# Float32 weights straight from the load for the second MoE's groups of 128 rows

## The chip, the cores and the metric

The kernel runs on one core of a Trainium2 chip. The metric is the device time of one execution in microseconds, the median of several runs; lower is better.

## The reference

Three layers stand one behind the other. The first is windowed attention with 4 batches, 8 heads, 576 positions and head size 64; its output is read as x with 2304 rows of 512. The second is a dense MoE layer, softplus(x @ w_in) @ w_out with an inner width of 2048. The third is a top-2 MoE with 8 experts of inner width 1024, and this is the one that the change is about:

```python
for e in range(E):
    for k in range(2):
        mask = top2[:, k] == e
        if not mask.any():
            continue
        h = np.maximum(x[mask] @ w1[e], 0.0)
        out[mask] += top2_w[mask, k, None] * (h @ w2[e])
```

`w1[e]` is 512 x 1024 and `w2[e]` is 1024 x 512, both float32, 2 MB each. Every row of x goes to its two best experts, weighted by `top2_w`.

## The kernel before

**Stages.** Attention is interleaved with the first MoE, which works through 9 chunks of 256 rows; each chunk is also routed (logits, top 2, rank in its expert's list), and each row's number and weight go into a table in DRAM, `rect`, by expert. Then the second MoE works through groups of rows that share an expert. A group of 256 rows is a *pair*, a group of 128 rows a *single*. There are 18 pairs (3 early ones and 15 late ones) and 5 singles that always run; two more singles stand under a condition at the end and do not run here. The order of the late ones is two pairs, a single, then three times three pairs and a single, then four pairs and the last single.

**Splitting.** To keep float32 precision, a matmul in the format float32r is done on split operands: a value is written as a high part, rounded to float32r, and a low part, the rest. high x high, high x low and low x high are added up: three matmuls for one product. Weights come by DMA as float32 into one of 4 raw buffers (`raw2`, 128 x 1024, 512 KB, `w2_load`); `w2_split` turns each into two ring tiles (`w_tile`, 128 x 2 x 512, 512 KB each). The high part of each half is copied by ACT (L1067), the low part is a subtraction (L1068), for the first half on POOL once the first MoE has freed its weights, for the second on DVE. The ring has 24 slots (`NRING`) of the same size as a raw buffer. A group needs 8 loads and so 16 ring tiles.

**A pair.** `g_rows` reads the group's part of `rect` (`rc`, L975, 4 buffers), `g_gather` fetches its rows with an indirect DMA from POOL's queue (`xg`, L984), `g_transpose` turns them over on TensorE (L199), ACT and DVE evict them as `xh` and `xl` (L999, L1000). For each of 8 steps f, `s1` makes one h tile of 128 x 256 (12 matmuls of 256 columns, the weights stationary), ACT and DVE evict it as `gh` and `gl` (L1100, L1101), and two steps later `s3` adds six matmuls of 512 columns to the two y (or z) tiles. At the end ACT and DVE evict these with the row weight as scale (`ys`, L1168, L1171), and POOL scatters them with an indirect DMA that adds to `out` (L1162), one DMA for each 128 rows.

**A single.** It has two steps of 512 columns. `s1` uses the transposed rows as the stationary operand and the weights as the moving one: 4 blocks of the contraction, 3 matmuls of 512 columns each, 12 in a step. ACT evicts h with the ReLU as `hs` (L1117), `s2` turns it over with 4 transposes, ACT and DVE split it into `th` and `tlo` (L1133, L1134), and `s3` adds 12 matmuls of 512 columns to y or z.

**What sets the order.** The program is written out in one order for each engine, by the class `Order`: TensorE's work is written down step by step, its cost is added to a planned time, and chains of steps for the other engines are put into their queues when the planned time reaches them. The costs in it are the author's figures and set the order alone. Each engine, and SP's queue of DMA issues, then works through its queue strictly in order. `pump` is called whenever a ring tile has been used up (`w2_free`): it loads while a raw buffer is free (`w2_load`), and splits while the ring has room for two tiles (`w2_split`). The pieces are taken in the order of the list `WJ`. A load into a raw buffer waits for the split of the piece that was in it, four pieces before; the high copy into a ring slot waits for the matmul that read it last. A row list `rc` waits for the scatter of the group four before it, which read the same buffer. PSUM has 2 h buffers, and the transposes share the t buffers with z.

The matmuls are all issued by one line, L188 in `mm`, so the groups of the profile are told apart by tiles: `h<-w,xh` with 512 columns is a single's up-projection, `y<-w,th` and `z<-w,th` its down-projection, `h<-xh,w` with 256 columns a pair's (or the first MoE's) up-projection.

Of the kernel before, what the change touches and what calls it, by code (L numbers as in the profile page):

```python
# [18 lines left out]
P = 128  # L19
# [76 lines left out]
def ca(n):  # L96
    return 0.06 + n * 0.000833
# [15 lines left out]
def moe_chain_kernel(ctx, tc, qk, v, w_in, w_out, w_gate, w_noise, noise, w1, w2, out):  # L113
# [875 lines left out]
    def g_transpose(g, a):  # L989
        n, eo, i = groups[g]  # L990
        d = GR[g]
        pt = ps_t(("gx", g, a)).rearrange("p (c t) -> p c t", c=KC)
        for kc in range(KC):
            tr(pt[:, kc, :], d["xg"][a][:, kc * P:(kc + 1) * P], ident)
        if a == 0:
            d["xT"] = tuple(tl(mid, [P, KC, CT], F32R, x, 2, ("gup", g)) for x in ("xh", "xl"))
        xh, xl = d["xT"]
        sl = slice(a * P, (a + 1) * P)
        chain(("A", ca(512), lambda: ACT.activation(xh[:, :, sl], pt, AF.Copy)),  # L999
              ("V", cv(512), lambda: DVE.tensor_sub(xl[:, :, sl], pt, f32(xh[:, :, sl])), ("gx", g, a)))  # L1000
# [3 lines left out]
    for g, (n, eo, i) in enumerate(groups):  # L1004
# [3 lines left out]
        else:  # L1008
            WJ += [(g, 0, f) for f in range(NF1 // 2)] + [(g, 1, f) for f in range(NF1 // 2)]
    NW = len(WJ)  # L1010
    wl, wsp = [0], [0]
    REG, W2, RAW2 = {}, {}, {}
    NRAW2 = 4
    freed = [0]
    nslot = [0]

    def w2_load():
        j = wl[0]
        if j >= NW or (j >= NRAW2 and ("w2", j - NRAW2) not in o_.fin):
            return False  # L1020
        g, kind, f = WJ[j]
        if g >= sure[0] or ("tab", int(g >= NEARLY)) not in o_.fin:
            return False
        wl[0] += 1
        n, eo, i = groups[g]
        if g not in REG:
            REG[g] = SP.value_load(TB[eo][0:1, 0, i:i + 1], min_val=0, max_val=E - 1)
            if g >= NEARLY:
                g_rows(g)
            chain(("P", 1.1 * n, lambda: g_gather(g), ("gg", g)), (None, 2.2, None, ("gl", g)), after=4.0)  # L1030
        e = bass.ds(REG[g], 1)
        raw = tl(p2, [P, 1024], F32, "raw2", NRAW2, ("w2", j))
        chain(("DMA", (1 << 19) / 330e3, None), (None, 2.0, None, ("r2", j)))
        if kind == 1:
            SP.dma_start(raw.rearrange("p (a n) -> p a n", a=2),
                         w2[e, f * 256:(f + 1) * 256, :].rearrange("e (a p) n -> p (e a) n", p=P))
        elif n == 2:
            SP.dma_start(raw.rearrange("p (c f) -> p c f", c=KC),
                         w1[e, :, f * 256:(f + 1) * 256].rearrange("e (c p) f -> p (e c) f", p=P))
        else:  # L1040
            h, c0 = divmod(f, 2)
            SP.dma_start(raw.rearrange("p (c f) -> p c f", c=2),
                         w1[e, c0 * 256:(c0 + 1) * 256, h * 512:(h + 1) * 512]
                         .rearrange("e (c p) f -> p (e c) f", p=P))
        RAW2[j] = raw
        return True

    def w2_split():
        j = wsp[0]
        if j >= wl[0] or sptr[0] < len(suses) or live1() + nslot[0] + 2 - freed[0] > NRING:  # L1050
            return False
        wsp[0] += 1
        nslot[0] += 2
        g, kind, f = WJ[j]
        n = groups[g][0]
        raw = RAW2.pop(j)
        for a in range(2):
            t = W2[g, kind, 2 * f + a] = w_tile()
            if kind == 0 and n == 2:
                src = raw.rearrange("p (c a f) -> p c a f", c=KC, a=2)[:, :, a, :]  # L1060
                hi, lo = (t[:, z].rearrange("p (c f) -> p c f", c=KC) for z in range(2))
            else:
                src, hi, lo = raw[:, a * 512:(a + 1) * 512], t[:, 0], t[:, 1]
            key = ("w2", j) if a else ("w2a", j)
            on_v = a or live1() > 0
            sub = ("V", cv(512)) if on_v else ("P", cg(512))
            chain(("A", ca(512), lambda hi=hi, src=src: ACT.activation(hi, src, AF.Copy), None, (("r2", j),)),  # L1067
                  sub + (lambda e=DVE if on_v else POOL, hi=hi, lo=lo, src=src: e.tensor_tensor(  # L1068
                      lo, src, f32(hi), OP.subtract), key))
        return True  # L1070
# [19 lines left out]
    def s1(g, f):  # L1090
        n = groups[g][0]
        if n == 2:
            need(("w2" if f % 2 else "w2a", WJ.index((g, 0, f // 2))))
            for a in range(2):
                need(("gx", g, a))
            ph = up(W2[g, 0, f], GR[g]["xT"], CT, ("hr2", g, f))
            w2_free()
            gh = tl(mid, [P, CT], F32R, "gh", 4, ("dn", g, f))
            gl = tl(mid, [P, CT], F32R, "gl", 4, ("dn", g, f))
            chain(("A", ca(CT), lambda: ACT.activation(gh, ph, AF.Relu)),  # L1100
                  ("V", cv(CT), lambda: DVE.scalar_tensor_tensor(gl, ph, 0.0, f32(gh), op0=OP.max, op1=OP.subtract),  # L1101
                   ("hr2", g, f)))
            H2[g, f] = (gh, gl)
        else:
            need(("gx", g, 0))
            ph = tl(psum, [P, 512], F32, "h", 2, ("hr2", g, f))
            xh, xl = GR[g]["xT"]
            x = 0
            for kc in range(KC):
                need(("w2" if kc % 2 else "w2a", WJ.index((g, 0, 2 * f + kc // 2))))  # L1110
                w = W2[g, 0, 4 * f + kc]
                for l, r in ((xh, 0), (xh, 1), (xl, 0)):
                    mm(ph, l[:, kc, :P], w[:, r, :], x == 0, x == 3 * KC - 1)
                    x += 1
                w2_free()
            hs = tl(p2, [P, 512], F32, "hs", 2, ("ht", g, f))
            chain(("A", ca(512), lambda: ACT.activation(hs, ph, AF.Relu), ("hr2", g, f)))  # L1117
            H2[g, f] = hs
        if f == (NF1 if n == 2 else 2) - 1:
            mark(("gup", g))  # L1120

    def s2(g, f):
# [5 lines left out]
        for x in range(4):  # L1128
            tr(pt[:, x, :], hs[:, x * P:(x + 1) * P], ident)
        mark(("ht", g, f))  # L1130
        th = tl(p2, [P, 4, P], F32R, "th", 2, ("dn", g, f))
        tlo = tl(p2, [P, 4, P], F32R, "tlo", 2, ("dn", g, f))
        chain(("A", ca(512), lambda: ACT.activation(th, pt, AF.Copy)),  # L1133
              ("V", cv(512), lambda: DVE.tensor_sub(tlo, pt, f32(th)), ("hT", g, f)))  # L1134
        H2[g, f] = (th, tlo)

    def s3(g, f):
        n = groups[g][0]
# [8 lines left out]
            w2_free()  # L1147
        else:
            need(("hT", g, f))
            th, tlo = H2.pop((g, f))  # L1150
            for x in range(4):
                ff = 4 * f + x
                need(("w2" if ff % 2 else "w2a", WJ.index((g, 1, ff // 2))))
                down(Y2[g], th[:, x, :], tlo[:, x, :], W2[g, 1, ff], ff == 0, ff == NF1 - 1)
                w2_free()
        mark(("dn", g, f))
        if f == (NF1 if n == 2 else 2) - 1:
            rc = GR[g]["rc"]
# [180 lines left out]
```

## Time and profile before

| | |
|---|---|
| median of 3 runs | 1256.97 us (1254.11 to 1257.41) |
| the profiled execution, its own time | 1252.39 us |
| its span, first to last instruction | 1250.5 us |
| mean granted TensorE clock | 0.948 |
| TensorE matmul, weight load | 1104.3 us (88%), 929.4 us (74%) |
| VectorE, ScalarE, GpSimd | 877.1 us (70%), 655.9 us (52%), 734.6 us (59%) |
| DMA | 237.19 MB, mean 190 GB/s |

The second MoE has TensorE to itself from about 700 us on; the last matmul ends near 1238 us. Busy shares are means over the whole program. In the profile PE is TensorE's matmuls and PEld its weight loads, DVE is VectorE, ACT ScalarE, POOL GpSimd and SP the queue that issues most DMAs. A line of time gives the start, the duration, the engine, the line of the kernel, the operation with its tiles, how many were merged, and in brackets how long the engine stood idle before it and what the profile takes for the cause. A group line gives the count, the busy time, the mean of one in ns, and the idle time before. Where a wait is put down to an engine that had long been done, another cause is meant, often a DMA.

### The profile page before, as it was taken

To read this page: it belongs to the slowest core of one execution; us is meant where nothing else is said; L and a number is where in the kernel's file an instruction comes from. 1 tells how busy PE (TensorE), PEld (TensorE's weight loads), DVE (VectorE), ACT (ScalarE), POOL (GpSimd) and SP (SyncE) were. 2 spreads that over 40 slices of the span, in tenths; PEclk is the share of its full clock that TensorE was granted. 3 is DMA by queue.
4 is the path that set the end of the run, shared out by engine and by line. 5 is a ranking of instruction groups with operands and counts; after the bars stand their busy time and mean duration, and the time that the engine had idled before them with its cause. 6 is when DMAs were issued, how large, how long until landed. Compare 5 with 4: busy or idle time off the path is not lost. (4 is left out here: it accounts for less than half of the span.)

```text
span 1250.5 us, 21557 instructions
## 1 busy us (share of the span) xinstructions
PE 1104.3 (88%) x7021; PEld 929.4 (74%) x7021; DVE 877.1 (70%) x2136; ACT 655.9 (52%) x1653; POOL 734.6 (59%) x718
## 2 busy tenths in 40 slices
PE   5567689998999999999998987987987988988996
PEld 3445467877878778888876887977977977977884
DVE  8999999675677776767588775755655655655671
ACT  6655455554545455555355534555655554654651
POOL 4666666455464646565554546666567566576661
PEclk8778879999999999999999998998998998998998
DMA  5465434367757555555585558678678677787762
GB/s 211 154 190 186 143 102 137 124 192 240 253 185 253 182 194 186 194 157 169 181 281 163 167 128 236 170 233 245 176 231 237 185 235 221 200 234 210 211 164 27
DMA packets 138068, 237.19 MB, mean 190 GB/s; under 512 B 18336, under 2 KB 73760, under 8 KB 137952
## 3 DMA queue, kind: packets, MB, share of 16 engines
q1 hardware_dynamic: 127616, 214.24, 53.6%
q0 software_dynamic: 10336, 21.54, 8.8%
q8 instruction: 57, 0.93, 0.3%
q14 instruction: 59, 0.48, 0.1%
HBM read 205.41 MB, written 30.33 MB: 189 GB/s over the span
## 5 line engine op out<-in xcount | busy, mean ns | idle before, releaser
L188 PE MATMUL h<-xh,w 128*128 128x256 f32 x2304 | 485.0, 293 | 63.0 <-DVE gl L1101 36.9
L188 PEld LDWEIGHTS h<-xh,w 128*128 128x128 f32 x2304 | 388.7, 196 | 95.5 <-DVE gl L1101 41.3
L1068 DVE TENSOR_TENSOR w<-raw,w 128x512 fp32r<-128x512 f32 x197 | 241.5, 1229 | 164.1 <-ACT w L1067 153.0
L188 PE MATMUL h<-xl,w 128*128 128x256 f32 x1152 | 333.1, 289 | 15.0 <-DVE xl L423 10.5
L1067 ACT ACTIVATE w<-raw 128x512 fp32r<-128x512 f32 x368 | 221.5, 627 | 157.8 <-DMA raw<-in_moe_w 105.9
L1068 POOL TENSOR_TENSOR w<-raw,w 128x512 fp32r<-128x512 f32 x171 | 234.8, 1443 | 89.5 <-ACT w L1067 86.1
L188 PE MATMUL y<-w,gh 128*128 128x512 f32 x736 | 243.8, 413 | 6.0 <-DVE gh L556 6.0
L188 PEld LDWEIGHTS h<-xl,w 128*128 128x128 f32 x1152 | 226.3, 196 | 24.2 <-DVE xl L423 11.3
L559 POOL TENSOR_TENSOR su<-sa,su 128x256 f32<-128x256 f32 x144 | 108.0, 750 | 120.2 <-DVE su L558 90.3
L188 PEld LDWEIGHTS y<-w,gh 128*128 128x128 f32 x736 | 127.7, 193 | 33.6 <-issue 8.2
L188 PE MATMUL y<-w,gl 128*128 128x512 f32 x368 | 146.1, 397 | 0.7 <-DVE gl L557 0.7
L551 ACT ACTIVATE sa<-h 128x256 f32<-128x256 f32 x144 | 54.7, 380 | 165.4 <-PE h L188 139.6
L1162 POOL DMA_INDIRECT out<-ys,rc x41 | 70.0, 1708 | 117.9 <-PE h L188 39.2
L188 PE MATMUL z<-w,gh 128*128 128x512 f32 x416 | 139.1, 417 | 0.0
L555 POOL TENSOR_TENSOR sl<-sl,su 128x256 f32<-128x256 f32 x144 | 110.2, 766 | 19.0 <-DVE sl L554 4.6
L556 DVE CAST gh<-sl 128x256 fp32r<-128x256 f32 x144 | 62.6, 435 | 76.1 <-POOL sl L555 76.1
L364 POOL TENSOR_TENSOR s<-s,st 128x512 f32<-128x512 f32 (+2 forms) x80 | 80.2, 1007 | 53.0 <-DVE st L361 25.0
L355 ACT ACTIVATE s<-s,st 128x256 f32<-128x256 f32 (+2 forms) x160 | 76.2, 478 | 62.5 <-DVE st L351 62.5
L1100 ACT ACTIVATE gh<-h 128x256 fp32r<-128x256 f32 x144 | 54.7, 380 | 93.2 <-PE h L188 65.3
L188 PE MATMUL z<-w,gl 128*128 128x512 f32 x208 | 84.2, 405 | 3.1 <-DVE gl L557 3.1
L188 PEld LDWEIGHTS y<-w,gl 128*128 128x128 f32 x368 | 70.4, 191 | 18.2 <-DVE gl L557 2.0
L557 DVE TENSOR_TENSOR gl<-sl,gh 128x256 fp32r<-128x256 f32 x144 | 81.6, 568 | 3.1
(235 smaller groups left out, 1646.1 us busy)
## 6 DMA issues: line engine op xcount, KB each, us to landing
raw<-in_moe_w SPq DMA_DIRECT2D x184, 512.0 KB, 4.8
w<-scratch SPq DMA_DIRECT2D x126, 512.0 KB, 4.7
qkT<-in_qk SPq DMA_DIRECT2D x20, 512.0 KB, 6.1
scratch<-w SPq DMA_DIRECT2D x18, 512.0 KB, 3.1
raw<-in_moe_w_in SPq DMA_DIRECT2D x16, 512.0 KB, 5.6
raw<-in_moe_w_out SPq DMA_DIRECT2D x16, 512.0 KB, 6.1
out<-zero SPq DMA_DIRECT2D x19, 256.0 KB, 6.0
x1buf<-x SPq DMA_DIRECT2D x9, 512.0 KB, 4.5
```

Of the source, the lines that this page charges most:

```text
L188: PE.matmul(o, l, r, start=start, stop=stop)
L355: ACT.activation(s[:nq, j, :n], s[:nq, j, :n], AF.Exp, bias=st[:nq, j:j + 1], scale=-1.0, accum_out=st[:nq, 2 + j:3 + j])
L364: POOL.tensor_tensor(s[:nq, :, :n], s[:nq, :, :n], st[:nq, 6:8, None].to_broadcast([nq, 2, n]), OP.mult)
L551: chain(("A", ca(CT), lambda: ACT.activation(a, ph, AF.Abs)), ("A", ca(CT), lambda: ACT.activation(a, a, AF.Exp, scale=-1.0), ("e", t)), ( ...
L555: ("P", cg(CT), lambda: POOL.tensor_add(l, l, u), None, (("d", t),)),
L556: ("V", cv2(CT), lambda: DVE.tensor_copy(gh, l)),
L557: ("V", cv(CT), lambda: DVE.tensor_sub(gl, l, f32(gh)), ("g", t)))
L559: ("P", cg(CT), lambda: POOL.tensor_tensor(u, a, u, OP.subtract), ("d", t)), after=2 * ca(CT) + 0.15)
L1067: chain(("A", ca(512), lambda hi=hi, src=src: ACT.activation(hi, src, AF.Copy), None, (("r2", j),)), sub + (lambda e=DVE if on_v else POOL ...
L1068: sub + (lambda e=DVE if on_v else POOL, hi=hi, lo=lo, src=src: e.tensor_tensor(lo, src, f32(hi), OP.subtract), key))
L1100: chain(("A", ca(CT), lambda: ACT.activation(gh, ph, AF.Relu)), ("V", cv(CT), lambda: DVE.scalar_tensor_tensor(gl, ph, 0.0, f32(gh), op0=O ...
L1162: POOL.indirect_dma_start(out=out[:, :], out_offset=bass.IndirectOffsetOnAxis(ap=rc[:, a, 0:1], axis=0), in_=ys, in_offset=None, compute_o ...
```

## The change

Singles no longer split anything. Their weights are loaded as float32 straight into a ring slot (`raws`), one slot for each of the 8 loads instead of a raw buffer and two slots, and TensorE reads them as they are. The gathered rows are evicted once, as float32 (`xs`), without `xl`; h likewise (`th` becomes float32, `tlo` is gone). Each block of the contraction is one float32 matmul instead of three in float32r: 4 instead of 12 in a step of `s1` and of `s3`. Pairs are computed as before.

The list of pieces is walked by `w2_load` and `w2_split` as before, but for a single `w2_load` only prepares the group (its expert's number, its row list, its gather) and issues no weight DMA; `w2_split` issues that when the ring has a slot. So `w2_load` can go past a single to the next pair, up to 12 pieces ahead of `w2_split`, and the four raw buffers count pairs' pieces only (`JP`, `PJ`). The loads of a single wait for the matmul that last read the slot.

```diff
 def g_transpose(g, a):
...
+        if n == 1:
+            d["xT"] = tl(p2, [P, KC, P], F32, "xs", 2, ("gup", g))
+            return chain(("A", ca(512), lambda: ACT.activation(d["xT"], pt, AF.Copy), ("gx", g, a)))
...
+    JP = [j for j in range(NW) if groups[WJ[j][0]][0] == 2]
+    PJ = {j: x for x, j in enumerate(JP)}
...
+    NAHEAD = 12
...
     def w2_load():
         j = wl[0]
-        if j >= NW or (j >= NRAW2 and ("w2", j - NRAW2) not in o_.fin):
+        if j >= NW or j >= wsp[0] + NAHEAD or (j in PJ and PJ[j] >= NRAW2 and ("w2", JP[PJ[j] - NRAW2]) not in o_.fin):
             return False
...
+        if n == 2:
+            w2_fetch(j, tl(p2, [P, 1024], F32, "raw2", NRAW2, ("w2", j)), ("r2", j))
+        return True
+
+    def w2_fetch(j, raw, key):
+        g, kind, f = WJ[j]
         e = bass.ds(REG[g], 1)
-        raw = tl(p2, [P, 1024], F32, "raw2", NRAW2, ("w2", j))
-        chain(("DMA", (1 << 19) / 330e3, None), (None, 2.0, None, ("r2", j)))
+        chain(("DMA", (1 << 19) / 330e3, None), (None, 2.0, None, key))
...
     def w2_split():
         j = wsp[0]
-        if j >= wl[0] or sptr[0] < len(suses) or live1() + nslot[0] + 2 - freed[0] > NRING:
+        if j >= wl[0] or sptr[0] < len(suses):
+            return False
+        g, kind, f = WJ[j]
+        n = groups[g][0]
+        if live1() + nslot[0] + n - freed[0] > NRING:
             return False
         wsp[0] += 1
-        nslot[0] += 2
-        g, kind, f = WJ[j]
-        n = groups[g][0]
+        nslot[0] += n
+        if n == 1:
+
+            raw = wpool.tile([P, 1024], F32, name="raws", tag="w", bufs=NRING)
+            w2_fetch(j, raw, ("w2", j))
+            return True
...
 def s1(g, f):
...
-            xh, xl = GR[g]["xT"]
-            x = 0
             for kc in range(KC):
-                need(("w2" if kc % 2 else "w2a", WJ.index((g, 0, 2 * f + kc // 2))))
-                w = W2[g, 0, 4 * f + kc]
-                for l, r in ((xh, 0), (xh, 1), (xl, 0)):
-                    mm(ph, l[:, kc, :P], w[:, r, :], x == 0, x == 3 * KC - 1)
-                    x += 1
-                w2_free()
+                j = WJ.index((g, 0, 2 * f + kc // 2))
+                need(("w2", j))
+                mm(ph, GR[g]["xT"][:, kc, :], RAW2[j][:, kc % 2 * 512:kc % 2 * 512 + 512], kc == 0, kc == KC - 1)
+                if kc % 2:
+                    del RAW2[j]
+                    w2_free()
...
 def s2(g, f):
...
-        th = tl(p2, [P, 4, P], F32R, "th", 2, ("dn", g, f))
-        tlo = tl(p2, [P, 4, P], F32R, "tlo", 2, ("dn", g, f))
-        chain(("A", ca(512), lambda: ACT.activation(th, pt, AF.Copy)),
-              ("V", cv(512), lambda: DVE.tensor_sub(tlo, pt, f32(th)), ("hT", g, f)))
-        H2[g, f] = (th, tlo)
+        th = tl(p2, [P, 4, P], F32, "th", 2, ("dn", g, f))
+        chain(("A", ca(512), lambda: ACT.activation(th, pt, AF.Copy), ("hT", g, f)))
+        H2[g, f] = th
...
 def s3(g, f):
...
-                need(("w2" if ff % 2 else "w2a", WJ.index((g, 1, ff // 2))))
-                down(Y2[g], th[:, x, :], tlo[:, x, :], W2[g, 1, ff], ff == 0, ff == NF1 - 1)
-                w2_free()
+                j = WJ.index((g, 1, ff // 2))
+                need(("w2", j))
+                mm(Y2[g][0], th[:, x, :], RAW2[j][:, x % 2 * 512:x % 2 * 512 + 512], ff == 0, ff == NF1 - 1)
+                if x % 2:
+                    del RAW2[j]
+                    w2_free()
```

The added lines move the line numbers: the copies and subtractions of `w2_split` are L1085 and L1086 in the changed kernel, the loads L1050 and L1047 for pairs and L1054 and L1047 for singles, `hs` L1133, `th` L1148, `gh` L1118, the scatter L1179.

More of the change, by code (lines that the diff above doesn't have):

```diff
@@ L1036, in w2_load @@
                          w2[e, f * 256:(f + 1) * 256, :].rearrange("e (a p) n -> p (e a) n", p=P))
-        elif n == 2:
+        elif groups[g][0] == 2:
             SP.dma_start(raw.rearrange("p (c f) -> p c f", c=KC),
@@ L1045, in w2_load @@
         RAW2[j] = raw
-        return True
     def w2_split():
         j = wsp[0]
-        if j >= wl[0] or sptr[0] < len(suses) or live1() + nslot[0] + 2 - freed[0] > NRING:
+        if j >= wl[0] or sptr[0] < len(suses):
[3 more added lines that the diff above has]
+        if live1() + nslot[0] + n - freed[0] > NRING:
             return False
         wsp[0] += 1
-        nslot[0] += 2
-        g, kind, f = WJ[j]
-        n = groups[g][0]
+        nslot[0] += n
[3 more added lines that the diff above has]
+            return True
         raw = RAW2.pop(j)
@@ L1058, in w2_split @@
             t = W2[g, kind, 2 * f + a] = w_tile()
-            if kind == 0 and n == 2:
+            if kind == 0:
                 src = raw.rearrange("p (c a f) -> p c a f", c=KC, a=2)[:, :, a, :]
@@ L1149, in s3 @@
             need(("hT", g, f))
-            th, tlo = H2.pop((g, f))
+            th = H2.pop((g, f))
             for x in range(4):
                 ff = 4 * f + x
-                need(("w2" if ff % 2 else "w2a", WJ.index((g, 1, ff // 2))))
-                down(Y2[g], th[:, x, :], tlo[:, x, :], W2[g, 1, ff], ff == 0, ff == NF1 - 1)
-                w2_free()
+                j = WJ.index((g, 1, ff // 2))
[4 more added lines that the diff above has]
+                    w2_free()
         mark(("dn", g, f))
```

## The prediction

> **What bounds the kernel now.** I read the page first, then the waits of TensorE in the second MoE, then the lines of time around one group of 128 rows.
>
> ```profile
> span 1250.5 us, 21557 instructions
> PE 1104.3 (88%) x7021; PEld 929.4 (74%) x7021; DVE 877.1 (70%) x2136; ACT 655.9 (52%) x1653; POOL 734.6 (59%) x718
> ```
>
> TensorE is the busiest engine, so the question is where it waits. The waits of TensorE between 671 and 1250 us (who waited for whom: us in total, times, longest), and one row for each of the longest:
>
> ```profile
> PE h L188 <- DVE gl L1101: 36.9, 10, 6.4
> PE t L199 <- DVE xl L1000: 11.5, 4, 3.5
> PE h L188 <- DVE xl L1000: 4.5, 4, 2.4
> 851.38 0.58 PE L188 MATMUL h<-xh,w 128*128 128x256 f32 x1 [6.45 <-DVE gl L1101]
> 946.66 0.58 PE L188 MATMUL h<-xh,w 128*128 128x256 f32 x1 [6.38 <-DVE gl L1101]
> 1043.58 0.58 PE L188 MATMUL h<-xh,w 128*128 128x256 f32 x1 [6.16 <-DVE gl L1101]
> 1139.20 0.58 PE L188 MATMUL h<-xh,w 128*128 128x256 f32 x1 [6.20 <-DVE gl L1101]
> 815.97 0.62 PE L188 MATMUL h<-w,xh 128*128 128x512 f32 x2
> 911.39 0.62 PE L188 MATMUL h<-w,xh 128*128 128x512 f32 x2
> 1223.53 0.61 PE L188 MATMUL h<-w,xh 128*128 128x512 f32 x2
> ```
>
> Matmuls h<-w,xh belong to groups of 128 rows alone, which I call singles; the others are pairs. A single starts at 815.97, the next at 911.39, the last at 1223.53. Four long waits of 6.2 to 6.45 us, 25.2 in all, each lie inside the pair that follows one of the first four singles; the four waits for transposes (11.5) lie inside those singles. So TensorE is held by its own work, except around the singles. What holds it there, first inside a single, then after it, and the median time of a scatter to landing:
>
> ```profile
> 819.74 1.15 ACT L1067 ACTIVATE w<-raw 128x512 fp32r<-128x512 f32 x2 [2.62 <-DMA raw<-in_moe_w]
> 823.96 0.58 ACT L1117 ACTIVATE hs<-h 128x512 f32<-128x512 f32 x1
> 826.38 0.66 PE L199 MATMUL t<-ident,hs 128*128 128x128 f32 x4 [2.53 <-DVE xl L1000]
> 833.91 1.88 POOL L1162 DMA_INDIRECT out<-ys,rc  x1 [0.17 <-issue]
> 840.43 1.58 POOL L1162 DMA_INDIRECT out<-ys,rc  x1 [4.64 <-PE h L188]
> 841.47 5.53 POOL L1068 TENSOR_TENSOR w<-raw,w 128x512 fp32r<-128x512 f32 x4
> 843.36 0.37 SPq L1038 DMA_DIRECT2D raw<-in_moe_w  x1
> 848.47 1.15 ACT L1067 ACTIVATE w<-raw 128x512 fp32r<-128x512 f32 x2 [9.00 <-DMA raw<-in_moe_w]
> 850.09 0.37 ACT L1100 ACTIVATE gh<-h 128x256 fp32r<-128x256 f32 x1
> out<-ys,rc POOLq DMA_INDIRECT x41, 5.7
> ```
>
> ACT works in order. A conversion that waits for its load keeps the eviction behind it waiting, and TensorE has only two h buffers. The load is late because it needs a raw buffer whose POOL half isn't converted; POOL stood before its second scatter (840.43), which waits for the first one's landing (833.91 plus some 5.7). Once per pair this happens; only after a single is nothing left in the ring to cover it.
>
> The clock falls with these waits (stage; busy time of each engine; granted clock, DMA share, GB/s):
>
> ```profile
> 840.00:844.00 4.00, 4.00 (x28) 3.65 (x27) 0.19 (x1) 0.00 (x0) 3.57 (x4) 1.00 0.38 40
> 848.00:852.00 4.00, 0.62 (x3) 0.63 (x4) 2.08 (x3) 3.53 (x8) 2.68 (x3) 0.56 0.91 308
> 852.00:856.00 4.00, 4.00 (x17) 3.65 (x17) 4.00 (x5) 2.21 (x5) 3.53 (x4) 0.58 0.97 201
> 1018.00:1022.00 4.00, 3.27 (x11) 2.34 (x11) 4.00 (x5) 3.90 (x8) 2.93 (x3) 0.65 0.73 224
> 1114.00:1118.00 4.00, 3.71 (x12) 2.85 (x13) 3.76 (x5) 3.52 (x7) 2.63 (x3) 0.59 0.86 225
> ```
>
> Busy time times what the clock lacks: 0.44 of 0.62 and 0.42 of 4.00 are 1.95 us after the long wait, 7.8 for four; 0.35 of 3.27 and 0.41 of 3.71 are 2.7 after two of the waits for transposes. The DMA engines moved 40 GB/s in the stage in which the loads were held, so they aren't the limit.
>
> **The change part by part.** *TensorE's own work.* In a single, 48 matmuls of fp32r become 16 of float32:
>
> ```order
> -L188 MATMUL h<-w,xh 128x512 x2
> -L188 MATMUL h<-w,xl 128x512
> -L188 MATMUL h<-w,xh 128x512 x2
> -L188 MATMUL h<-w,xl 128x512
> -L188 MATMUL h<-w,xh 128x512 x2
> -L188 MATMUL h<-w,xl 128x512
> -L188 MATMUL h<-w,xh 128x512 x2
> -L188 MATMUL h<-w,xl 128x512
> +L188 MATMUL h<-raws,xs 128x512 x4
> ```
>
> That is TensorE at one half of a single's up-projection. Where twelve stood, four stand; the down-projection (y<-raws,th) changes alike. Their prices (the first row is where the twelve of 1223.53 end):
>
> ```profile
> 1226.25 0.61 PE L188 MATMUL y<-w,gh 128*128 128x512 f32 x2
> L188 PE MATMUL t<-x1T,wgn 128*32 128x256 f32 x72 | 9.5, 388 | 0.0
> 694.60 0.59 PE L188 MATMUL t<-x1T,wgn 128*32 128x256 f32 x2
> 818.70 0.60 PE L199 MATMUL t<-ident,xg 128*128 128x128 f32 x4
> L199 PE MATMUL t<-ident,xg 128*128 128x128 f32 x164 | 24.5, 272 | 0.0
> L199 PEld LDWEIGHTS t<-ident,xg 128*128 128x128 f32 x164 | 19.3, 140 | 1.1
> ```
>
> Twelve take 1226.25 - 1223.53 = 2.72 us, 0.227 each, 10.9 for 48. A full float32 matmul of this shape isn't in the trace; the nearest is the router's, 4 for each of 9 chunks in the code and 72 in the record: each is two instructions. The last two of a chunk span 0.59, one lasts 0.38 to 0.39, so the second starts 0.21 after the first; 256 columns take 0.21, 512 take 0.43, the two instructions 0.85. Sixteen are 13.7 us; with the 0.014 that an fp32r matmul takes beyond 512/256 of 0.1067 (0.227 against 0.213), for each of 32 instructions, 14.1. So a single grows by 3.2, five by 16.0. Lower end: no such extra, 13.8. Upper end: the 32 weight loads aren't hidden; by the transposes' row, 0.140 each is 4.5 per single, 38 in all with the rest. I take 16.0, since the transposes hide theirs: four in 0.60, one lasting 0.27, start every 0.11, faster than a load of 0.14.
>
> The Trainium skill ("TensorE: Matmul & The Clock Gate", Weight-path perf modes and LDWEIGHTS) says that the fast weight load is off for FP32 and that a load costs its columns over 1.2 GHz, 107 ns here, which speaks against the change: unhidden, 32 a single would by that estimate add 3.4 us, 17 over five singles. The rows of the transposes speak for hiding; no run so far shows it for this shape.
>
> *Conversions.* Gone for five singles: 80 halves on ACT, about 80 on DVE and POOL, and the small splits of xg and of hs.
>
> ```profile
> L1067 ACT ACTIVATE w<-raw 128x512 fp32r<-128x512 f32 x368 | 221.5, 627 | 157.8 <-DMA raw<-in_moe_w 105.9
> L1068 POOL TENSOR_TENSOR w<-raw,w 128x512 fp32r<-128x512 f32 x171 | 234.8, 1443 | 89.5 <-ACT w L1067 86.1
> SPq L1038 <- POOL w L1068: 67.4, 24, 9.2
> ```
>
> The third row is SP's wait for raw buffers. That is 80 x 0.63 = 50 us of ACT, 40 x 1.44 = 58 of POOL and the other 40 halves on DVE; in itself worth nothing, since none of the three ends last. What it frees is the cover: a single's load takes one ring slot instead of two, and no raw buffer. 24 slots then hold the single (8) and the whole next pair (16). ACT's queue around a single's first eviction, before (raw2_11218 to raw2_11336 are pieces 3 to 7 of the next pair):
>
> ```order
> L1067 ACTIVATE w_11323<-raw2_11218 128x512
> L1067 ACTIVATE w_11324<-raw2_11218 128x512
> L1067 ACTIVATE w_11338<-raw2_11249 128x512
> L1067 ACTIVATE w_11339<-raw2_11249 128x512
> L1067 ACTIVATE w_11352<-raw2_11280 128x512
> L1067 ACTIVATE w_11353<-raw2_11280 128x512
> L1117 ACTIVATE hs_11354<-h_11325 128x512
> L999 ACTIVATE xh_11363<-t_11355 128x4x128
> L1067 ACTIVATE w_11401<-raw2_11311 128x512
> ```
>
> and the same place now (raw2_11145 is the next pair's last piece, raw2_11196 the first of the pair after that):
>
> ```order
> L1085 ACTIVATE w_11256<-raw2_11145 128x512
> L1085 ACTIVATE w_11257<-raw2_11145 128x512
> L1133 ACTIVATE hs_11258<-h_11241 128x512
> L1002 ACTIVATE xh_11267<-t_11259 128x4x128
> L1085 ACTIVATE w_11284<-raw2_11196 128x512
> ```
>
> At the single's first eviction, five pieces of the next pair were converted; now it is all eight. A piece feeds one step of a pair:
>
> ```profile
> 838.68 0.28 PE L188 MATMUL h<-xh,w 128*128 128x256 f32 x1
> 841.50 0.28 PE L188 MATMUL h<-xh,w 128*128 128x256 f32 x1
> ```
>
> A step is 841.50 - 838.68 = 2.82 us, so three pieces are 8.5 us of stock, more than the 6.4 that the late load cost; and neither POOL nor ACT has the single's own halves in front of them any more. I count the waits as gone: 25.2 and 11.5, with the slow clock 7.8 and 2.7: 47.2. Small waits for xl stay (4.5); I leave 3.2 for new ones, about 0.8 at each of four singles, the size that these have beside their longest (4.5 - 2.4 over three is 0.7). Ends: 0, and the 11.5 that the transposes lose now.
>
> *SP's queue.* The row list of the pair after a single is now loaded before the single's weights:
>
> ```order
> L975 DMA rc_10778<-rect_115 128x2x2
> L1050 ISA
> L1050 DMA raw2_10780<-in_moe2_w1 128x4x256
> L1047 ISA
> L1047 DMA raw2_10816<-in_moe2_w2 128x2x512
> L1050 ISA
> L1050 DMA raw2_10860<-in_moe2_w1 128x4x256
> L1047 ISA
> L1047 DMA raw2_10891<-in_moe2_w2 128x2x512
> L1054 ISA
> L1054 DMA raws_10893<-in_moe2_w1 128x2x512
> ```
>
> (rc_10778 is that pair's list, four of its pieces follow, then the single's first load; before, the list stood behind all eight loads of the single.) There are four such lists, so this one waits until the group four back has scattered. That group ends when the third back begins on TensorE. From its end to the landing of its second scatter: the trace has 1.9 for the first, 5.7 to land, 1.6, 5.7 again, near 15 us. Behind it SP holds four pieces of the pair and the single's eight. These are 6.3 MB; at the 200 to 308 GB/s of the stages above they take 20 to 31 us, so they have landed by 35 to 46 us. A pair takes 8 x 2.82 and two groups of transposes (4 x 0.11 each), 23 us, so the single is due after 46, its last load later still. It fits, with the first loads some 15 us early. Each single load also waits for a slot that TensorE frees, which comes before that too.
>
> *Sum.* 1252.4 (the profiled execution, 1.9 beyond its span) - 47.2 + 16.0 + 3.2 = 1224.4, a change of -28.0. That execution lies 4.6 under the median of the three runs, 1257.0; from there it is 1229.0. I take 1227.
>
> **The rivals.** *The late load remains by half.* POOL's blocked scatter isn't touched, the loads of a pair still hang on it, and ACT may still stand before one once per single. For it: the 4.64 us wait recurs with every pair. Against it: the stock of converted pieces. Half of 25.2 + 7.8 comes back, 16.5: 1243.
>
> *The gap after a single stays whole,* since its cause is POOL's scatter. Only the waits inside the single and their clock (14.2) go: -14.2 + 16.0 + 3.2 = +5 at most, +2 without new waits: by the same step to the median as the forecast's 1257 to 1260, about as before.
>
> *Slower: the single comes late.* SP stands at the row list until POOL's scatter has landed, the single's loads behind it reach their slots after TensorE is there, and TensorE waits w and then runs about 2 us slowly. From 47.2 - 16.0 = 31 us over four singles, it decides once w passes 31/4 - 2 = 6 us, which needs the loads some 20 us later than I count; with w = 10 the time is 1252.4 - 31 + 4 x 12 = 1269, 1272 by the forecast's step to the median. For it: SP already waits up to 9.2 us for POOL at one load, and the list puts a wait of its own there. Against it: the 15 us in hand.
>
> *The weight loads aren't hidden* (the page's rule above, with the transposes' 0.140): 38 instead of 16, 1249. Or the float32 matmuls don't do what the code says and run in one pass each, 0.43 us: 16 take 7, a gain of 4 each, 1191 or so; the two records per matmul speak against it.
>
> **How the numbers follow.** Forecast, own range 1216 to 1238: 0.61. Half remains: 0.15. Gap whole: 0.08, three quarters of it within measurement. Single late: 0.09. Loads unhidden: 0.05. One pass: 0.02. The low end, 1214, is 1227 without the extra (2.2), the new waits (3.2) and the waits for xl (4.5), and 3 for the spread of the three runs (1254.1 to 1257.4). The high end, 1250, takes in the half that remains and the unhidden loads. A measurement of this kernel tells about 0.3%, 3.8 us, from no change. Faster: 0.61 + 0.15 + 0.05 + 0.02 = 0.83, less 0.01 for the unhidden loads at their upper end, which goes to no change; same 0.06 + 0.01 = 0.07; slower 0.09 + 0.02 = 0.11.
>
> **What would show it.** Right: no wait near 6 us in the pairs after singles, no wait of 2 to 3.5 before t<-ident,hs, a single's four float32 matmuls starting 0.88 apart, about 88 us from single to single instead of 95.4, a clock of 1.0 there. Wrong: TensorE waiting for raws, four matmuls over 4.5 us, SP standing at the row list for much over 15 us, or long waits of ACT for raw2 that still end in TensorE's.

## The result and the profile after

The changed kernel takes 1220.42 us (median of 4 runs, 1217.62 to 1223.33), the kernel before in the same comparison 1257.19 (4 runs, 1254.11 to 1258.73). The ratio is 0.9723 with a 95% interval of 0.9694 to 0.9751. The forecast was 1227.0 with a range of 1214 to 1250.

The profiled execution took 1223.05 us, 2.6 above the median of its four; that of before, 1252.39, lies below all four of before here. So the two traces differ by 29.3 us and the medians by 36.8. What follows from the traces is measured against 29.3.

The head of the page after:

```profile
span 1221.1 us, 21110 instructions
PE 1109.4 (91%) x6941; PEld 909.2 (74%) x6941; DVE 819.6 (67%) x2081; ACT 617.4 (51%) x1573; POOL 679.2 (56%) x678
```

TensorE has 5.1 us more busy time in a span that is 29.4 shorter, and ACT, DVE and POOL each have 38 to 58 us less. First the starts of the five singles, in the lines of time of TensorE. Of the kernel before, the third and the fourth, which stand beside the 815.97, 911.39 and 1223.53 shown above:

```profile
1006.82 0.62 PE L188 MATMUL h<-w,xh 128*128 128x512 f32 x2
1103.13 0.61 PE L188 MATMUL h<-w,xh 128*128 128x512 f32 x2
```

and of the changed one:

```profile
816.47 3.70 PE L188 MATMUL h<-raws,xs 128*128 128x512 f32 x8 [1.51 <-DVE gl L1119]
903.59 3.70 PE L188 MATMUL h<-raws,xs 128*128 128x512 f32 x8 [1.20 <-DVE gl L1119]
990.85 3.70 PE L188 MATMUL h<-raws,xs 128*128 128x512 f32 x8 [1.09 <-DVE gl L1119]
1078.36 3.70 PE L188 MATMUL h<-raws,xs 128*128 128x512 f32 x8 [0.67 <-DVE gl L1119]
1192.73 3.60 PE L188 MATMUL h<-raws,xs 128*128 128x512 f32 x8
```

Up to the first single nothing is gained (815.97 before, 816.47 now). From single to single it is 87.1, 87.3 and 87.5 us where it was 95.4, 95.4 and 96.3, and 114.4 to the last one instead of 120.4. From there to the end it is 28.4 instead of 27.0. That is the 29.3, and it lies in the four stretches between singles.

The waits of TensorE from 780 us on, in the kernel before (us in total, times, longest):

```profile
PE h L188 <- DVE gl L1101: 26.0, 6, 6.4
PE t L199 <- DVE xl L1000: 11.5, 4, 3.5
PE h L188 <- DVE xl L1000: 2.1, 3, 1.0
```

and in the changed one:

```profile
PE h L188 <- DVE gl L1119: 6.0, 5, 1.6
PE h L188 <- DVE xl L1003: 3.9, 3, 2.7
```

39.6 us have become 9.9. No wait is longer than 2.7, and the four for transposes are gone. What is left is small and partly new: four of the five waits for gl stand at the start of a single (the 0.67 to 1.51 in the lines above). The second stretch from single to single (busy time of PE, PEld, DVE, ACT, POOL; granted clock, DMA share, GB/s), before:

```profile
911.40:1006.80 95.40, 85.59 (x517) 75.95 (x516) 56.51 (x68) 52.51 (x102) 60.92 (x46) 0.96 0.75 212
930.00:950.00 20.00, 13.62 (x78) 12.10 (x77) 6.99 (x9) 8.01 (x17) 12.81 (x10) 0.85 0.75 188
```

and after (the second row of each is the time around the first pair that follows the single):

```profile
903.60:990.90 87.30, 85.94 (x501) 71.38 (x501) 46.47 (x57) 45.83 (x88) 50.11 (x38) 1.00 0.81 237
925.00:945.00 20.00, 20.00 (x132) 18.17 (x131) 16.53 (x15) 11.98 (x23) 15.84 (x13) 1.00 0.86 231
```

TensorE's idle time falls from 9.8 to 1.4 us (95.40 - 85.59 and 87.30 - 85.94). Its busy time rises by only 0.35, since the slower float32 is nearly paid for by the clock, which is 1.00 instead of 0.96. The difference, 8.1, is what the starts show for this stretch. The second rows show the place: 6.4 of 20 us were idle around that pair, and none is now.

### The profile page after: what moved, and what is told of

It is laid out like the page before. It is cut to its first block, busy times and chain, and to the rows that moved or that the text cites. A ratio compares the mean times of both kernels' runs of the same rounds, so it can differ in the third digit from the quotient of the medians.

```text
span 1221.1 us, 21110 instructions
## 1 busy us (share of the span) xinstructions
PE 1109.4 (91%) x6941; PEld 909.2 (74%) x6941; DVE 819.6 (67%) x2081; ACT 617.4 (51%) x1573; POOL 679.2 (56%) x678
## 5 line engine op out<-in xcount | busy, mean ns | idle before, releaser
L188 PE MATMUL h<-xl,w 128*128 128x256 f32 x1152 | 331.6, 288 | 16.9 <-DVE xl L423 10.5
L1086 DVE TENSOR_TENSOR w<-raw,w 128x512 fp32r<-128x512 f32 x157 | 191.4, 1223 | 136.6 <-ACT w L1085 131.1
L1085 ACT ACTIVATE w<-raw 128x512 fp32r<-128x512 f32 x288 | 176.7, 629 | 112.6 <-DMA raw<-in_moe_w 47.2
L1086 POOL TENSOR_TENSOR w<-raw,w 128x512 fp32r<-128x512 f32 x131 | 176.6, 1459 | 75.4 <-ACT w L1085 74.6
L1179 POOL DMA_INDIRECT out<-ys,rc x41 | 71.8, 1752 | 137.4 <-DMA raws<-in_moe_w 31.2
L1118 ACT ACTIVATE gh<-h 128x256 fp32r<-128x256 f32 x144 | 55.1, 383 | 143.1 <-PE h L188 114.4
L1119 DVE SCALAR_TENSOR_TENSOR gl<-h,gh 128x256 fp32r<-128x256 f32 x144 | 60.3, 419 | 79.8 <-ACT gh L1118 76.4
```

The costliest lines, as they stand in the source:

```text
L188: PE.matmul(o, l, r, start=start, stop=stop)
L1179: POOL.indirect_dma_start(out=out[:, :], out_offset=bass.IndirectOffsetOnAxis(ap=rc[:, a, 0:1], axis=0), in_=ys, in_offset=None, compute_o ...
```

## The experiments

The theory of the prediction is that the saved *space* (one ring slot instead of two, no raw buffer) gives a stock of converted pieces that covers POOL's stand before its second scatter. The experiments set two rivals beside it: that the *relief* of ACT, DVE and POOL does it, and that TensorE's float32 work or SP's stand at the row list takes part of the gain back. Each kernel was compared with the kernel before on the same chip.

### The space taken back

The changed kernel, but a single's load is charged two slots; the second is allocated and never written.

```diff
-        if live1() + nslot[0] + n - freed[0] > NRING:
+        if live1() + nslot[0] + 2 - freed[0] > NRING:
...
-        nslot[0] += n
+        nslot[0] += 2
...
             raw = wpool.tile([P, 1024], F32, name="raws", tag="w", bufs=NRING)
+            wpool.tile([P, 1024], F32, name="spare", tag="w", bufs=NRING)
...
                     del RAW2[j]
+                    freed[0] += 1
                     w2_free()
```

> The changed kernel, but each load of a single is charged two ring slots again, as the split pair of tiles was; nothing else of the change is undone (no splitting, float32 matmuls). If the gain came from the stock in the ring (the theory of the prediction), about half of the next pair is no longer held while a single runs and waits of 2 to 6 us come back at four singles: 1232 to 1252 us, ratio to the kernel before 0.98 to 0.997. If it came from the conversions that ACT, DVE and POOL no longer do, nothing is lost: 1217 to 1225, ratio 0.97 to 0.976.

Measured: 1236.96 us, ratio 0.9833 (0.9789 to 0.9878). Its waits of TensorE from 780 us on, and one of the four:

```profile
PE h L188 <- DVE gl L1120: 15.5, 4, 4.7
```

```profile
940.30 0.58 PE L188 MATMUL h<-xh,w 128*128 128x256 f32 x1 [4.66 <-DVE gl L1120]
```

The four waits in the pairs after singles are back, at 3.5 to 4.7 instead of 6.2 to 6.45 us, and a stretch takes 90.7 to 92.7. The stock is that of the kernel before again: by the count of copies on ACT, five pieces of the next pair are converted at the first single's first eviction there (90 copies `w<-raw`, 80 of them for the five pairs up to the single), as in the kernel before (106, with 16 for the single), and eight in the changed kernel (96). So the ring slots are a cause, worth some 14 (by the ratios) to 16.5 us (by the medians). But some 20 of the 36.8 stay without them, and so do the waits for transposes: none is back. What is left in this kernel of the change is that a single's halves are no longer converted, that it passes by the raw buffers, and that row list and gather of the next pair are issued earlier.

### The relief taken back

The changed kernel, with the 80 copies and 80 subtractions of the singles done all the same, into a spare tile that nobody reads.

```diff
+            for a in range(2):
+                hi = lo = p2.tile([P, 512], F32R, name="spare", bufs=3)
+                src = raw[:, a * 512:(a + 1) * 512]
+                on_v = a or live1() > 0
+                sub = ("V", cv(512)) if on_v else ("P", cg(512))
+                chain(("A", ca(512), lambda hi=hi, src=src: ACT.activation(hi, src, AF.Copy), None, (("w2", j),)),
+                      sub + (lambda e=DVE if on_v else POOL, hi=hi, lo=lo, src=src: e.tensor_tensor(
+                          lo, src, f32(hi), OP.subtract), ("du", j, a)))
```

> The changed kernel, with the 80 high copies and 80 low subtractions of the singles' weights done again, from the raw weights into a spare tile that nobody reads; loads, ring slots and matmuls as in the change. If the gain is the stock in the ring, it stays but for small waits: 1218 to 1230, ratio 0.969 to 0.979. If it is the engines' freed time (or ACT no longer standing before a single's loads), most is lost: 1238 to 1258, ratio 0.985 to 1.0.

Measured: 1295.75 us, 1.0307 (1.0261 to 1.0354), beyond what any theory gave. The same was run with all the added subtractions on DVE (`on_v = True` in these lines), so that POOL has none of them:

> The changed kernel with the singles' 80 high copies and 80 low subtractions done again into a spare tile, as in the second experiment, but all 80 subtractions on DVE and none on POOL; the pairs' first halves stay on POOL. If it was POOL's queue that cost 75 us there, the time returns to 1215 to 1230, ratio 0.967 to 0.978. If ACT's copies standing before the single's loads cost it, it stays at 1270 to 1300, ratio 1.01 to 1.035.

Measured: 1282.71 us, 1.0201 (1.0154 to 1.0249). One row of ACT's waits in each, the first run:

```profile
ACT spare L1078 <- DMA raws<-in_moe_w: 53.7, 6, 13.5
```

and the second:

```profile
ACT spare L1078 <- DMA raws<-in_moe_w: 53.7, 11, 13.0
```

ACT stands 53.7 us for the single's loads in both, with the pairs' evictions behind it: a load that has to wait for the ring slot that TensorE frees now has a copy waiting for it in ACT's queue, which neither of the two kernels compared has. So both runs have a new stand of ACT in them beside the old work, and on the relief they decide nothing. That this stand is what makes them slower is argued from these rows; no run takes it away alone.

### POOL's part, in both kernels

If POOL's queue is what makes the conversions late, taking its subtractions away should help the kernel *before*, too, with all its splitting left in. One line, in the kernel before:

```diff
-            on_v = a or live1() > 0
+            on_v = True
```

> The kernel before, with every low half subtracted on DVE, none on POOL. If the waits after a single come from raw buffers whose POOL half stands behind a scatter, the four waits of 6.2 to 6.5 us and their slow clock (33 us) go, less a little for DVE's added 170 subtractions: 1222 to 1235, ratio 0.972 to 0.983. If the ring's space was the cause and POOL only happened to be late, they stay: 1250 to 1262, ratio 0.995 to 1.004.

Measured: 1197.32 us, 0.9518 (0.9475 to 0.9561), some 25 us below the range expected if POOL's halves are the cause, and faster than the changed kernel. One stretch of it, from single to single:

```profile
898.00:980.60 82.60, 82.60 (x517) 74.32 (x516) 59.45 (x101) 53.92 (x103) 19.62 (x14) 1.00 0.85 249
```

TensorE is busy 82.6 of 82.6 us at a clock of 1.00, and it has no wait over 0.5 us left after 780. All the splitting is still there, on ACT and DVE; only POOL's share has left POOL's queue. With it go not only the four waits after singles and their slow clock, but the waits inside singles too: a stretch is 12.8 us shorter than the 95.4 before. The prediction had ACT stand before late loads; this wait of ACT from 780 us on, in the kernel before,

```profile
ACT w L1067 <- DMA raw<-in_moe_w: 94.8, 42, 9.4
```

in the changed kernel,

```profile
ACT w L1085 <- DMA raw<-in_moe_w: 35.7, 23, 5.2
```

and in the kernel before with the subtractions on DVE:

```profile
ACT w L1067 <- DMA raw<-in_moe_w: 22.4, 17, 2.5
```

Moved subtractions alone take away more of ACT's waits for loads than the change does. (The sum of these waits does not rank kernels by itself; the run with five raw buffers below shows it.)

Is it the scatter, or simply the time of the subtractions? In the kernel before, with the subtractions left on POOL, the second scatter of each pair is left out (the rows of the second half don't get that expert's part):

```diff
-                    POOL.indirect_dma_start(
+                    if a == 0:
+                        POOL.indirect_dma_start(
```

> The kernel before, with the second scatter of each pair left out (the rows of its second half don't get this expert's part); evictions, subtractions on POOL and everything else stay. With all subtractions off POOL the kernel before ran without a wait from single to single. If it is the standing before the second scatter (4 to 6 us a pair) that held POOL's subtractions and so the loads, the cycle of three pairs and a single falls from 95.4 to 83 to 87 us: 1205 to 1222, ratio 0.958 to 0.972. If it is the time of POOL's own subtractions (1.44 us each), only the 1.7 us of the scatter itself goes: 1245 to 1256, ratio 0.99 to 0.999.

Measured: 1201.83 us, 0.9549 (0.9506 to 0.9592), a little below the range expected for the scatter. Its waits of TensorE from 780 us on:

```profile
PE h L188 <- DVE gl L1101: 4.8, 8, 1.3
```

The long waits are gone though POOL still makes every subtraction it made. A scatter left out is also less for the DMA engines to move and an earlier end of each group; but with the subtractions moved all scatters stay, and the waits are gone as well. What the two edits share is that no subtraction stands behind a wait between two scatters. So that stand, with the conversions queued behind it, is the cause, as the prediction named it. The same edit in the changed kernel:

> The changed kernel, with the second scatter of each pair left out in the same way. The changed kernel's cycle is 87.2 us, that with POOL free of subtractions 85.4. If the scatter's standing is what is left: 85.4 to 86, 1208 to 1214, ratio 0.96 to 0.966. If POOL's own work is: no gain, 1217 to 1224.

Measured: 1212.20 us, 0.9621 (0.957 to 0.9672), with this first stretch:

```profile
818.55:903.91 85.36, 85.36 (x501) 71.39 (x500) 38.10 (x57) 45.60 (x87) 45.91 (x36) 1.00 0.77 232
```

TensorE has no idle time left in it. What the stand still costs the changed kernel is thus about 2 us in a stretch (87.1 to 87.5 less 85.4).

A further raw buffer alone does not cure the kernel before. The kernel before with `NRAW2 = 5`:

> The kernel before, with five raw buffers instead of four: one more load under way. If late loads that hold ACT are what TensorE waits for, one load more in flight takes 2 to 3 us off each of the eight waits at singles: 1230 to 1248, ratio 0.979 to 0.993. If only space for converted tiles counts, or POOL's standing still is longer than one more load covers, 1250 to 1260, ratio 0.995 to 1.003.

Measured: 1255.64 us, 0.9992 (0.9969 to 1.0016), median of 10 runs; the profiled execution, 1248.7, is the fastest of them. Its waits of TensorE for gl from 671 us on, and ACT's for loads from 780 us on:

```profile
PE h L188 <- DVE gl L1101: 42.7, 17, 6.2
ACT w L1067 <- DMA raw<-in_moe_w: 35.4, 15, 7.2
```

Before, the first row was 36.9 us in 10. The four waits for transposes (11.5) are gone here, and waits of 1.7 to 3.6 at the starts of singles have come; after singles TensorE still stands for 3.9 to 6.2. ACT's waits for loads are down from 94.8 to 35.4, as low as in the changed kernel, and the time has not moved. POOL's and DVE's lines ahead of the wait of 5.1 us that ends at 944.06:

```profile
935.35 1.59 POOL L1162 DMA_INDIRECT out<-ys,rc  x1 [5.88 <-DMA out<-ys,rc]
936.39 6.72 POOL L1068 TENSOR_TENSOR w<-raw,w 128x512 fp32r<-128x512 f32 x5
936.42 7.25 DVE L1068 TENSOR_TENSOR w<-raw,w 128x512 fp32r<-128x512 f32 x1 [3.58 <-ACT w L1067]
```

A load can land earlier, but its POOL half still stands behind the scatter, and one subtraction on DVE lasts as long as POOL's five, with the eviction gl behind it. So one raw buffer more is no cure; more than five were not tried.

### The price of float32, and what is behind it

The changed kernel, with every second block of the contraction left out in singles (`s1` and `s3`), so 8 instead of 16 float32 matmuls in each:

```diff
-                mm(ph, GR[g]["xT"][:, kc, :], RAW2[j][:, kc % 2 * 512:kc % 2 * 512 + 512], kc == 0, kc == KC - 1)
+                if kc % 2 == 0:
+                    mm(ph, GR[g]["xT"][:, kc, :], RAW2[j][:, :512], kc == 0, kc == KC - 2)
...
-                mm(Y2[g][0], th[:, x, :], RAW2[j][:, x % 2 * 512:x % 2 * 512 + 512], ff == 0, ff == NF1 - 1)
+                if x % 2 == 0:
+                    mm(Y2[g][0], th[:, x, :], RAW2[j][:, :512], ff == 0, ff == NF1 - 2)
```

> The changed kernel, with every second block of the contraction left out in singles (two float32 matmuls in a step instead of four; the result lacks half of each sum); loads, slots and evictions as in the change. If TensorE is what bounds the program from the first single on, each single falls by half of 16 x 0.86, 6.9 us: five are 34, so 1184 to 1192, ratio 0.943 to 0.95. If loads, conversions or scatters bound it (a cycle of three pairs and a single needs 16.8 MB of weights), waits take the place of the matmuls: 1200 to 1220, ratio 0.955 to 0.972.

Measured: 1221.08 us, 0.9727 (0.9681 to 0.9773): no gain, though 40 matmuls of 0.86 us, 34.4 us of TensorE's work, are out (the planned times shrink with them). Its waits from 780 us on, and one stretch:

```profile
PE h L188 <- DVE xl L1003: 13.3, 3, 4.5
PE h L188 <- DVE gl L1119: 11.1, 12, 2.5
```

```profile
909.00:996.10 87.10, 81.11 (x484) 69.21 (x484) 47.14 (x57) 43.56 (x87) 50.09 (x38) 0.98 0.80 236
```

The stretch is still 87.1 us; waits have taken the place of the work. So the changed kernel seems to have two limits close together, TensorE's own work and a supply of about 87 us from single to single. To see TensorE's alone, the changed kernel with `on_v = True`:

> The changed kernel, with every low half subtracted on DVE, none on POOL. If POOL's scatters still cost something through the raw buffers (waits of 0.7 to 5.9 us are left on TensorE, 24 in all in this stage), 5 to 15 us are gained: 1205 to 1215, ratio 0.96 to 0.967. If the stock already covers them, the same: 1217 to 1224.

Measured: 1210.37 us, 0.9621 (0.9591 to 0.9651), 85.4 us in each of three stretches, with no wait over 0.5 us from 780 on. And both edits in one, subtractions on DVE and half of the float32 matmuls:

> The changed kernel with all subtractions on DVE and every second block of the contraction left out in singles, as in the fifth experiment, where that gave nothing. If POOL's queue was the second limit there, right behind TensorE, TensorE now shows: the cycle falls by 16 x 0.43 = 6.9 from 85.4 to 78.5, 1174 to 1184, ratio 0.934 to 0.943. If the loads themselves are the limit, it stays: 1205 to 1212.

Measured: 1185.65 us, 0.9429 (0.9386 to 0.9472), stretches of 79.1, 80.0 and 79.3. Now TensorE's work counts: 24.7 us less, though not all of the 34.4 and not the 6.9 a stretch that was expected (5.3 to 6.3). So the supply that bounds the changed kernel is POOL's, as the run with one scatter says too.

The price of float32 itself comes from the two kernels that TensorE alone bounds: 85.4 - 82.7 = 2.7 us in each of the three stretches (108.8 - 106.1 = 2.7 in the longer last one), and 1210.4 - 1197.3 = 13.1 over the five singles (13.0 by the ratios; the two ran on different chips).

### SP's stand at the row list

Two more buffers for the row lists, `"rc", 6` instead of `"rc", 4`, in the changed kernel, and once more together with the subtractions on DVE:

> The changed kernel, with six buffers for row lists instead of four, so that the list of the pair after a single need not wait for the scatter of the group four back. SP's waits at L975 (39.7 us in six) go. If the prediction's account holds, that standing still is covered by converted pieces and the time stays: ratio 0.968 to 0.975. If the change paid for its new order with it, 4 to 10 us are gained: ratio 0.963 to 0.968.

Measured: 1223.89 us, 0.9733 (0.9687 to 0.978), as the changed kernel.

> Both: six row lists, and all subtractions on DVE. If the two waits stand one behind the other (SP for the list, then POOL for the raw buffers), together they give more than the sum of the two alone; if each is covered, no more than the better one.

Measured: 1210.89 us, 0.9626 (0.9598 to 0.9654), as the changed kernel with the subtractions on DVE. In SP's queue of the changed kernel the stand is there (its waits at the list from 780 us on, then the lines of time):

```profile
SPq L975 <- DMA out<-ys,rc: 39.7, 6, 10.2
860.39 0.37 SPq L1047 DMA_DIRECT2D raw<-in_moe_w  x1
862.13 12.37 SPq L975 DMA_DIRECT2D rc<-rect  x2
874.77 0.37 SPq L1050 DMA_DIRECT2D raw<-in_moe_w  x1
...
881.60 2.60 SPq L1054 DMA_DIRECT2D raws<-in_moe_w  x4
```

The 12.37 us hold two row lists, the single's and the next pair's; SP waits up to 10.2 for a scatter to land, and the single's loads start at 881.60, still 22 us ahead of the single at 903.59. Taking the stand away gains nothing in the medians. The two traces don't settle it: with six buffers the time from the first single to the last is 370.2 us instead of 376.3, most of it in the last stretch (109.9 instead of 114.4), but that execution is 8.6 later already at the router's last matmuls (701.94 instead of 693.33), ahead of the late groups. With POOL's subtractions on DVE the stretches are the same with four buffers and six. So the stand is covered there, and whether it costs the changed kernel a few us stays open.

## Why the prediction was right, and where it was not

**The cause and the place: right.** The four waits of 6.2 to 6.45 us and those for transposes went; with the small ones that are left or new, TensorE waits 29.7 us less from 780 on (39.6 - 9.9), and the clock is 1.00 in the stretches. The prediction put the cause in POOL's stand before the second scatter, and the kernel before with one scatter (1201.8) and with the subtractions on DVE (1197.3) shows it. In the changed kernel POOL stands there as before:

```profile
829.08 1.88 POOL L1179 DMA_INDIRECT out<-ys,rc  x1 [0.16 <-issue]
836.70 1.58 POOL L1179 DMA_INDIRECT out<-ys,rc  x1 [5.74 <-PE y L188]
837.74 4.34 POOL L1086 TENSOR_TENSOR w<-raw,w 128x512 fp32r<-128x512 f32 x3
```

It is idle for 5.74 us before the second scatter, and three subtractions come in a row behind it. So the rival "the gap stays whole" had its premise right, the cause untouched, and fell because the gap is now covered, in part by the stock. "Half remains" fell with the waits: none is over 2.7.

**The size.** The forecast was 88 us from single to single, and 87.1 to 87.5 were measured; its sum was -28.0 between profiled executions, and they differ by -29.3. The median came out 6.6 under the forecast: 1.3 is the sum, 2.6 the step up to the median that I added, and 2.6 that this profiled execution, unlike the one before, lies above its median. That the sum came within 1.3 is partly luck. Waits were to fall by 36.7 less 3.2 new ones, 33.5, and fell by 29.7; float32 was to cost 16.0 and costs 13 to 14.5; what is left for the clock and the rest is by subtraction 12.7 to 14.1 instead of 10.5. The errors nearly cancel.

**The step that failed: "in itself worth nothing, since none of the three ends last".** This was said of the conversions taken from ACT, DVE and POOL, and the forecast put what the change gains down to the stock of converted pieces. POOL did end last in the kernel before, not by busy time (59% of the span) but by its order: with its subtractions moved and nothing else changed, that kernel gains 60 us. And the stock is not the whole of the gain: with the ring slots taken back it is five pieces again, as before, and some 20 of the 36.8 us stay, the waits for transposes among them. That the missing conversions gave these 20 is not shown. They may as well come from the raw buffers that singles pass by, which the prediction named beside the slots, or from the order of the next pair's row list and gather; the two runs meant to tell them apart measured something else. What is known is that the stock of pieces alone, as the prediction counted it, carries 14 to 16.5 us, and that the forecast came out near the truth because it took all the waits as gone, whichever part of the change did it. (That no halves of the single stand in POOL's and ACT's queues any more, it names as well, without a price.)

**The float32 term, +16.0: too large by 1.5 to 3, and not a term of a sum.** The eight instructions of a step, and the tile's own row (shortest, median, longest ns):

```profile
908.95 3.60 PE L188 MATMUL h<-raws,xs 128*128 128x512 f32 x8
```

```profile
L188 PE MATMUL h<-raws,xs x80: 590/592/697, 816.5 to 1200.5; 128*128 128x512 f32 x80
```

Eight instructions span 3.60, one lasts 0.592, so the other seven start (3.60 - 0.592)/7 = 0.430 apart: 0.86 for a float32 matmul, not the 0.88 with the extra of fp32r. (The 0.1067 us for 256 columns in that extra is in no row; a pair's twelve matmuls of 256 columns start 0.119 apart, from 838.68 to 840.11.) Sixteen are 13.8, 2.9 more than before, the lower end given; the comparison of kernels says 2.7 and 13.1 in all. That is twice the 0.43 of "one pass", which is refuted. The weight loads are hidden, as the transposes' rows had suggested: their group

```profile
L188 PEld LDWEIGHTS h<-raws,xs 128*128 128x128 f32 x80 | 14.8, 189 | 21.0 <-issue 14.4 <-DVE gl L1119 6.2
```

has 0.189 us for each, and 0.430 from one instruction to the next is what the router's rows gave for the 512 columns by themselves, 0.43, so the load adds nothing. The rule that spoke against the change (the Trainium skill, "TensorE: Matmul & The Clock Gate", Weight-path perf modes and LDWEIGHTS: no fast load for FP32, 107 ns for 128 columns) thus costs nothing here; the record of a load is longer than that figure, 189 ns, and is covered all the same. And the term does not simply add: half of the float32 matmuls taken out gains nothing in the changed kernel. Its stretch is near the longer of TensorE's 85.4 and the supply's 87.

**SP's queue: right as to the single.** The prediction's "near 15 us" ran from a group's end to the landing of its second scatter; SP's own wait is 10.2 at most. The first loads, counted as landed some 15 us early, were issued 22 us ahead (the traces give no time of landing for them), and no wait of TensorE for raws is in its list. So the single does not come late, and the slower rival did not occur.

**The better version.** The kernel before with every subtraction on DVE takes 1197.3 us, 0.9518 (0.9475 to 0.9561). It keeps the cheaper float32r in singles and takes the conversions out from behind the scatters; the change covers that stand and pays for it with float32 matmuls, 13 us where TensorE is the limit.

## What to carry to other kernels

Look for what an in-order queue stands behind before taking work off it: here a queue at 59% busy set the pace because two scatters to one tensor stood in it with the weights' conversions behind them. When a wait is covered instead of removed, the next limit can be close behind, as here (85.4 and 87); halving the work of the engine that seems to bind (and once more with the suspected queue freed) told in two runs which of them it was. Redone dummy work is a poor test of relief if it brings a wait of its own into a queue.

## What the runs showed of the hardware

The subtraction on DVE (128 x 512, two inputs from SBUF) is slower on average beside POOL's subtractions than without them. A group of the kernel before, and the shortest, median and longest in it (ns):

```profile
L1068 DVE TENSOR_TENSOR w<-raw,w 128x512 fp32r<-128x512 f32 x197 | 241.5, 1229 | 164.1 <-ACT w L1067 153.0 <-issue 10.7
L1068 DVE TENSOR_TENSOR w<-raw,w x197: 670/768/4993, 642.1 to 1216.0; 128x512 fp32r<-128x512 f32 x197
```

and of the same kernel with all of them on DVE:

```profile
L1068 DVE TENSOR_TENSOR w<-raw,w 128x512 fp32r<-128x512 f32 x368 | 248.8, 695 | 67.1 <-ACT w L1067 58.5 <-issue 0.2
L1068 DVE TENSOR_TENSOR w<-raw,w x368: 668/692/1259, 644.3 to 1161.8; 128x512 fp32r<-128x512 f32 x184
```

The mean falls from 1229 to 695 ns, so 171 more of them cost DVE only 7.3 us. The median falls from 768 to 692 alone: some subtractions get very long, up to 4993, while half of them take no more than 768. The Trainium skill ("SBUF — State Buffer", SBUF: two separate sides) says that DVE and GpSimd share a port pair as an exclusive lock, held for a whole instruction, when a DVE operation with two SBUF inputs meets a GpSimd operation that reads SBUF; these rows agree, and the subtraction of 7.25 us beside POOL's five in the run with five raw buffers too. In the kernel before it is not what made TensorE wait: DVE was idle ahead of the long waits, as ahead of the one that ends at 851.38,

```profile
849.65 1.34 DVE L1068 TENSOR_TENSOR w<-raw,w 128x512 fp32r<-128x512 f32 x1 [9.46 <-ACT w L1067]
```

and with one scatter left out DVE's mean is nearly what it was, and the long waits are gone all the same:

```profile
L1068 DVE TENSOR_TENSOR w<-raw,w 128x512 fp32r<-128x512 f32 x197 | 232.8, 1186 | 115.1 <-ACT w L1067 102.8 <-issue 11.4
```
